# The end of the last block: the last half row is finished in two free banks, a quarter of a row each, with its earlier sum and x added ahead

## Chip, core and metric

One core of a Trainium2 chip. The metric is the device time of one execution in microseconds; the kernel before takes 622.09 us (median of the first three runs, 622.07 to 624.6). Each run also has a profile whose span is about 1.4 us shorter than its time. One run alone of a kernel on one core has the state "unknown"; kernels that were timed in several runs have the state "fast".

## The reference

```
xn = layernorm(x)                                   # x: [1, 2048, 1024] bf16
h_t = Lam_bar * h_(t-1) + B_bar xn_t                # a complex recurrence over 2048 steps
y   = 2 Re(C h) + xn * Dskip
act = a * tanh(softplus(a)),  a = xn w1 + b1        # w1: 1024 x 3584, w2: 3584 x 1024
out = x + y + act w2
```

## The kernel before

The rows are worked through in four blocks of 512. At the end of a block, `tail` sums the dense part (`act w2`) and the projection (`Re(C h)`) of eight *units* in the eight PSUM banks (the memory that TensorE sums into): unit u is row tile q = u//2 (128 rows) and half h = u%2 (512 of 1024 columns). The last steps of the projection (j = 5, 6, 7 with two components, so six matmuls a unit) are done row tile by row tile, so that VectorE can add x to a finished one and ScalarE's queue can store it while TensorE works on the next. In the last block the last row tile is finished in two halves: unit 6, then unit 7.

```python
        for j in range(NJ - njt):                       # the earlier steps, all units
            for ci in range(2):
                for u in range(8):
                    proj(j, ci, u, False)
        # ... cut
        def finish(q, lo, hi):
            # ... cut: src is one bank, or two as one row
            vop(lambda e: e.tensor_tensor(xr, src, xr, op=ALU.add), reads=b_src + [b_x], writes=[b_x])
            sem = s_out[i][q] if hi - lo > TB else DmaSem(nc, "d_end%d" % lo)
            out_events[i, q, lo] = AC.dma(lambda e: e.dma_start(out[0, r0:r0 + P, lo:hi], xr), sem, reads=[b_x])

        for q in range(NQ):
            units = [(2 * q, 2 * q + 1)]
            if blk == NB - 1 and q == NQ - 1:
                units = [(2 * q,), (2 * q + 1,)]        # the last row tile: unit 6, then unit 7
            for us in units:
                for j in range(NJ - njt, NJ):
                    for ci in range(2):
                        for u in us:
                            proj(j, ci, u, j == NJ - 1 and ci == 1)
                if len(us) == 1:
                    finish(q, (us[0] % 2) * TB, (us[0] % 2 + 1) * TB)
            if len(units) == 1:
                finish(q, 0, D)
```

`vop`, `PE.mm` and `AC.dma` put an instruction on the queue of VectorE, TensorE or ScalarE, with the waits that its data need. VectorE's queue runs in the order in which the program fills it.

## Time and profile before

In all views PE is TensorE (PEld its weight loads), DVE VectorE, ACT ScalarE, POOL GpSimd and SP SyncE; a q behind an engine means its queue. In a chain of waits, "issue" is time in which the engine waited for nothing that the profile shows; elsewhere in this text an *issue* is the work of a queue to start one transfer, and *landing* the moment when that transfer is reported complete.

The lines below are from the page of the kernel before: the span, each engine's busy time with its share, and the chain that ended last, by engine.

```profile
span 620.4 us, 7332 instructions
...
PE 613.4 (99%) x2905; PEld 287.6 (46%) x2961; DVE 465.6 (75%) x687; ACT 244.7 (39%) x158; POOL 49.9 (8%) x47
...
PE 96%; ACT 2%; DVE 1%; issue 1%; POOL 0%; DVEq 0%; POOLq 0%
```

TensorE is busy nearly all of the time. A change at the end of the last block can only touch what follows TensorE's last result. The next fence is the timeline from 616 us (start, duration, engine, line, operation, output<-inputs, shape, count; in brackets the engine's idle time before it and what ended it).

```profile
615.36 1.99 DVE L758 TENSOR_TENSOR xx<-ps,xx 128x1024 bf16<-128x1024 f32 x2 [1.36 <-PE ps L721]
615.80 2.10 PE L721 MATMUL ps<-CT,hT 128*128 128x512 bf16 x9
616.02 1.39 PEld L721 LDWEIGHTS ps<-CT,hT 128*128 128x128 bf16 x7
616.61 2.39 ACTq L760 DMA_DIRECT2D out_dram<-xx  x3
617.95 0.69 DVE L758 TENSOR_TENSOR xx<-ps,xx 128x512 bf16<-128x512 f32 x1 [0.60 <-PE ps L721]
```

The first line merges two adds: that of the third row tile (615.36, 1.22 us) and unit 6's (616.65, 0.69 us). Then VectorE is idle for 0.60 us until TensorE has finished unit 7, and adds its 512 columns from 617.95 to 618.64. The chain of waits ends the same way, with matmuls and then one add:

```profile
614.08 3.85 PE ps L721 x17
617.92 0.02 issue
617.95 0.69 DVE xx L758
```

The last two stores in the view of the issuing line (duration of the issue in ns, min/median/max; then time from the issue to landing):

```profile
L760 ACTq DMA_DIRECT2D out_dram<-xx x2: 339/339/339, 617.4 to 618.7; - x2
...
DMA to landing us min/median/max: 1.7/1.7/1.7
```

So the end is: last matmul result, 0.69 us of add, 0.03 us, 1.70 us of store (0.34 us of it the issue; the trace has landing at 620.37 for an issue at 618.67). The **tail**: from the start of the third row tile's add, which that row's last matmul releases, to the end of the span. Before, 620.412 - 615.356 = 5.06 us.

One more line of this profile is of use, from the timeline at the kernel's start: matmuls of 256 columns, of which the change will make twelve. 56 of them take 6.36 us; less the 0.27 us of one, that is 55 spacings of 111 ns on average (in the trace nearly all are 109 ns, and one is 183).

```profile
14.12 6.36 PE L502 MATMUL ps<-xnT,ring 128*128 128x256 bf16 x56
```

### The profile page before, as it was taken

What the parts mean: (1) busy time and instruction counts of PE and PEld (TensorE: products, weight loads), DVE (VectorE), ACT (ScalarE), POOL (GpSimd) and SP (SyncE); (2) the same over time, 40 slices, a digit from 0 to 9 for tenths busy, and PEclk for the clock granted to TensorE, in tenths of its full rate; (3) what the DMA queues carried; (4) which work ended last, traced back from release to release, by engine and by line L of the source; (5) the groups of instructions that cost most, each with busy time, mean ns of one, the idle gap of its engine ahead of it and who ended that gap; (6) DMA issues with size and microseconds to landing.
All of it is one profiled execution on the core that took longest, in us unless ns stands there. A gap on an engine that the chain in (4) does not pass through costs nothing.

```text
span 620.4 us, 7332 instructions
## 1 busy us (share of the span) xinstructions
PE 613.4 (99%) x2905; PEld 287.6 (46%) x2961; DVE 465.6 (75%) x687; ACT 244.7 (39%) x158; POOL 49.9 (8%) x47
## 2 busy tenths in 40 slices
PE   8999999999999999999999999999999999999998
PEld 8544444444444444444444444444444444444443
DVE  6899999999467599998147659999624856999603
ACT  5679995441079940000009992000001999000000
POOL 1998000000100000000010000000000000000000
PEclk9999999999999999999999999999999999999999
DMA  9999967740464301763065420285204542033001
GB/s 261 244 292 277 204 132 206 202 136 0 157 182 141 132 1 36 220 186 103 17 189 165 140 100 1 92 215 163 75 35 136 167 139 69 1 128 111 1 0 69
DMA packets 124332, 79.41 MB, mean 128 GB/s; under 512 B 48906, under 2 KB 106762, under 8 KB 124298
## 3 DMA queue, kind: packets, MB, share of 16 engines
q1 hardware_dynamic: 120800, 71.58, 42.4%
q10 hardware_dynamic: 2538, 4.21, 1.9%
q0 software_dynamic: 960, 3.15, 1.6%
q8 instruction: 24, 0.39, 0.3%
q14 instruction: 10, 0.08, 0.0%
HBM read 63.19 MB, written 4.19 MB: 109 GB/s over the span
## 4 chain that ended last, share of the span: by engine, by line
PE 96%; ACT 2%; DVE 1%; issue 1%; POOL 0%; DVEq 0%; POOLq 0%
PE ps L721 49%; PE ps L644 26%; PE ps L664 18%; PE ps L502 2%; PE ps L462 1%; ACT act L624 1%; ACT act L622 1%; ACT act L623 1%; DVE hb L651 0%; DVE act L629 0%; PE ps L383 0%; ACT L623 0%; DVE xx L436 0%; DVE xx L758 0%; DVE mt L434 0%
## 5 line engine op out<-in xcount | busy, mean ns | idle before, releaser
L721 PE MATMUL ps<-ring,act 128*128 128x512 bf16 x880 | 193.2, 379 | 0.8
L644 PE MATMUL ps<-xnT,ring 128*128 128x512 bf16 x832 | 182.7, 379 | 0.8
L622 ACT ACTIVATE act<-hb 128x3584 bf16<-128x3584 bf16 x16 | 50.9, 3183 | 244.2 <-DVE hb L651 243.7
L721 PEld LDWEIGHTS ps<-ring,act 128*128 128x128 bf16 x896 | 87.6, 98 | 105.8 <-DVE mt L669 0.3
L644 PEld LDWEIGHTS ps<-xnT,ring 128*128 128x128 bf16 x848 | 83.0, 98 | 99.8
L651 DVE TENSOR_SCALAR hb<-ps,par 128x512 bf16<-128x512 f32 x112 | 82.7, 747 | 55.1 <-PE ps L644 53.8
L664 PE MATMUL ps<-xnT,BT 128*128 128x512 bf16 x500 | 110.5, 379 | 0.6
L721 PE MATMUL ps<-CT,hT 128*128 128x512 bf16 x500 | 110.5, 379 | 0.6
L669 DVE TENSOR_TENSOR mt<-ps,tab 128x1024 bf16<-128x1024 f32 x64 | 75.3, 1219 | 13.3 <-PE ps L664 11.7
L664 PEld LDWEIGHTS ps<-xnT,BT 128*128 128x128 bf16 x512 | 50.1, 98 | 60.4
L721 PEld LDWEIGHTS ps<-CT,hT 128*128 128x128 bf16 x512 | 50.1, 98 | 60.4
L758 DVE TENSOR_TENSOR xx<-ps,xx 128x1024 bf16<-128x1024 f32 (+1 forms) x17 | 19.5, 1160 | 70.2 <-PE ps L721 70.1
L687 DVE TENSOR_TENSOR_SCAN hT<-cs,qi,hT 128x512 bf16<-128x512 f32 x48 | 58.9, 1268 | 0.0
L624 ACT ACTIVATE act<-act 128x3584 bf16<-128x3584 bf16 x16 | 51.0, 3190 | 0.2
L623 ACT ACTIVATE act<-act 128x3584 bf16<-128x3584 bf16 x16 | 51.0, 3190 | 0.2
L692 DVE TENSOR_TENSOR mt<-hT,tab 128x1024 bf16<-128x1024 bf16 x64 | 41.4, 688 | 1.1
L629 DVE TENSOR_TENSOR act<-act,hb 128x3584 bf16<-128x3584 bf16 x16 | 32.3, 2018 | 1.3 <-ACT act L624 1.3
L287 POOL DMA_DIRECT2D xx<-in_A_x_dram x12 | 6.7, 559 | 253.1 <-DVE xx L758 248.6
L598 ACT ACTIVATE ct<-CT,cs 128x512 f32<-128x512 bf16 x16 | 11.5, 718 | 28.8 <-DVE CT L600 24.5
L623 ACT ACT_TABLE_LOAD x16 | 20.5, 1283 | 0.3
L624 ACT ACT_TABLE_LOAD x16 | 20.5, 1283 | 0.3
L687 DVE TENSOR_TENSOR_SCAN hT<-cs,hT 128x512 bf16<-128x512 f32 x16 | 18.7, 1208 | 0.0
(78 smaller groups left out, 277.2 us busy)
## 6 DMA issues: line engine op xcount, KB each, us to landing
ring<-in_B_w_dram SPq DMA_DIRECT2D x112, 512.0 KB, 3.9
out_dram<-xx ACTq DMA_DIRECT2D x15, 256.0 KB, 2.1
xx<-in_A_x_dram POOLq DMA_DIRECT2D x12, 256.0 KB, 4.5
xx<-in_A_x_dram SPq DMA_DIRECT2D x3, 256.0 KB, 4.8
xx<-in_A_x_dram SPq DMA_DIRECT2D x2, 128.0 KB, 2.2
dsk<-in_A_Dskip_dram SPq DMA_DIRECT2D x1, 256.0 KB, 7.0
out_dram<-xx ACTq DMA_DIRECT2D x2, 128.0 KB, 1.7
xnT<-xn SPq DMA_TRANSPOSE x12, 4.5
```

Of the source, the lines that this page charges most:

```text
L622: aop(lambda e: e.activation(a, hs, AF.Exp), reads=[b_hb[g % 2]], writes=[b_act[g]])
L623: aop(lambda e: e.activation(a, a, AF.Ln, bias=1.0), reads=[b_act[g]], writes=[b_act[g]])
L624: aop(lambda e: e.activation(a, a, AF.Tanh), reads=[b_act[g]], writes=[b_act[g]])
L629: vop(lambda e: e.tensor_tensor(a, a, hs, op=ALU.mult), reads=[b_act[g], b_hb[g % 2]], writes=[b_act[g]])
L644: PE.mm(lambda e, k=k: e.matmul(ps[:, bank, :], lhsT=wt[:, k, fi * P:(fi + 1) * P], rhs=xnT[:, k, :], start=k == 0, stop=k == NK - 1), rea ...
L651: vop(lambda e: e.tensor_scalar(hb[:, hs, :], ps[:, bank, :], b1(f), None, op0=ALU.add), reads=[b_ps[bank], b_par], writes=[b_hbf[hs]])
L664: PE.mm(lambda e, j=j, ci=ci, k=k, bank=bank: e.matmul(ps[:, bank + ci, :], lhsT=BT[:, ci, j, k, :], rhs=xnT[:, k, :], start=k == 0, stop= ...
L669: vop(lambda e, s=s, u=u, j=j: e.tensor_tensor(mt[:, s, :, :], u, tab[:, s, j, :].unsqueeze(1).to_broadcast([P, 2, TB]), op=ALU.mult), rea ...
L687: vop(lambda e, ci=ci, init=init: e.tensor_tensor_scan(out=hT[:, ci, j, :], data0=cj("r", j).to_broadcast([P, TB]), data1=hT[:, ci, j, :], ...
L692: vop(lambda e, s=s: e.tensor_tensor(mt[:, s, :, :], hT[:, :, j, :], tab[:, s, j, :].unsqueeze(1).to_broadcast([P, 2, TB]), op=ALU.mult), ...
L721: PE.mm(lambda e: e.matmul(ps[:, u, :], lhsT=lhsT, rhs=rhs, start=st_, stop=last), reads=reads, writes=[b_ps[u]], first=st_, last=last)
L758: vop(lambda e: e.tensor_tensor(xr, src, xr, op=ALU.add), reads=b_src + [b_x], writes=[b_x])
```

## The change

The intent is to have less to do after the last matmul. Unit 7's sum so far (all but the last six matmuls) and x are added by VectorE into an f32 scratch tile. The last six steps go to banks 0 and 1, which are free by then, as two quarters of 256 columns: six matmuls for the first, six for the second. Each quarter is added to its part of the scratch and stored by itself, so only the second quarter's add and store follow the last matmul.

```diff
-                    proj(j, ci, u, False)
+                    proj(j, ci, u, blk == NB - 1 and u == 7 and j == NJ - njt - 1 and ci == 1)
 # ... cut
+        ends = blk == NB - 1
         for q in range(NQ):
+            units = (2 * q, 2 * q + 1) if not (ends and q == NQ - 1) else (2 * q,)
+            for j in range(NJ - njt, NJ):
+                for ci in range(2):
+                    for u in units:
+                        proj(j, ci, u, j == NJ - 1 and ci == 1)
+            finish(q, 0, len(units) * TB)
+        if ends:
+            tmp, b_tmp = ct[0]
+            b_x = b_xx[i][3].parts[1]
+            vop(lambda e: e.tensor_tensor(tmp[:], ps[:, 7, :], xx[:, i, 3, TB:D], op=ALU.add),
+                reads=[b_ps[7], b_x], writes=[b_tmp])
+            for h in range(2):
+                lo = TB + 256 * h
+                # ... six matmuls of 256 columns into bank h (cut)
+                vop(lambda e, h=h, lo=lo: e.tensor_tensor(
+                    xx[:, i, 3, lo:lo + 256], ps[:, h, 0:256], tmp[:, 256 * h:256 * h + 256], op=ALU.add),
+                    reads=[b_ps[h], b_tmp], writes=[b_end[h]])
+                out_events["end", h] = AC.dma(...)      # 64 KB (cut)
```

More of the change, by code (lines that the diff above doesn't have):

```diff
@@ L714, in build_kernel @@
     out_events = {}
+    b_end = [Buf("end%d" % h) for h in range(2)]
     def tail(blk):
@@ L732, in proj, with proj_quarter @@
             acc(u, hT[:, ci, j, q * P:(q + 1) * P], CT[:, ci, j, h * TB:(h + 1) * TB], [b_hT[ci][j], b_CT[j]], last)
+        def proj_quarter(j, ci, bank, lo, st_, last):
+            PE.mm(lambda e: e.matmul(ps[:, bank, 0:256], lhsT=hT[:, ci, j, 3 * P:4 * P], rhs=CT[:, ci, j, lo:lo + 256],
+                                     start=st_, stop=last),
+                  reads=[b_hT[ci][j], b_CT[j]], writes=[b_ps[bank]], first=st_, last=last)
         njt = 1 if blk == 0 else 3
@@ L746, in tail, with store @@
                 for u in range(8):
-                    proj(j, ci, u, False)
+                    proj(j, ci, u, blk == NB - 1 and u == 7 and j == NJ - njt - 1 and ci == 1)
         i = blk % 2
+        def store(q, lo, hi, sem):
+            r0 = blk * TB + q * P
+            b_x = b_xx[i][q] if hi - lo > TB else b_xx[i][q].parts[lo // TB]
+            out_events[i, q, lo] = AC.dma(lambda e: e.dma_start(out[0, r0:r0 + P, lo:hi], xx[:, i, q, lo:hi]),
+                                          sem, reads=[b_x])
@@ L750, in finish @@
         def finish(q, lo, hi):
+            bank, n = 2 * q + lo // TB, (hi - lo) // TB
+            b_x = b_xx[i][q] if n > 1 else b_xx[i][q].parts[lo // TB]
             xr = xx[:, i, q, lo:hi]
-            bank, r0 = 2 * q + lo // TB, blk * TB + q * P
-            b_x = b_xx[i][q].parts[lo // TB] if hi - lo <= TB else b_xx[i][q]
-            if hi - lo > TB:
-                src, b_src = ps[:, bank:bank + 2, :].rearrange("p a t -> p (a t)"), b_ps[bank:bank + 2]
-            else:
-                src, b_src = ps[:, bank, lo % TB:lo % TB + hi - lo], b_ps[bank:bank + 1]
@@ L758, in finish @@
-            vop(lambda e: e.tensor_tensor(xr, src, xr, op=ALU.add), reads=b_src + [b_x], writes=[b_x])
-            sem = s_out[i][q] if hi - lo > TB else DmaSem(nc, "d_end%d" % lo)
-            out_events[i, q, lo] = AC.dma(lambda e: e.dma_start(out[0, r0:r0 + P, lo:hi], xr), sem, reads=[b_x])
-        for q in range(NQ):
-            units = [(2 * q, 2 * q + 1)]
-            if blk == NB - 1 and q == NQ - 1:
-                units = [(2 * q,), (2 * q + 1,)]
-            for us in units:
+            src = ps[:, bank:bank + n, :].rearrange("p a t -> p (a t)")
@@ new lines, in finish @@
+            vop(lambda e: e.tensor_tensor(xr, src, xr, op=ALU.add), reads=b_ps[bank:bank + n] + [b_x], writes=[b_x])
+            store(q, lo, hi, s_out[i][q])
+        ends = blk == NB - 1
+        for q in range(NQ):
+            units = (2 * q, 2 * q + 1) if not (ends and q == NQ - 1) else (2 * q,)
[4 more added lines that the diff above has]
+            finish(q, 0, len(units) * TB)
@@ L767, in tail @@
+        if ends:
[5 more added lines that the diff above has]
+                lo = TB + 256 * h
                 for j in range(NJ - njt, NJ):
                     for ci in range(2):
-                        for u in us:
-                            proj(j, ci, u, j == NJ - 1 and ci == 1)
@@ L771, in tail @@
-                if len(us) == 1:
-                    finish(q, (us[0] % 2) * TB, (us[0] % 2 + 1) * TB)
-            if len(units) == 1:
-                finish(q, 0, D)
+                        proj_quarter(j, ci, h, lo, j == NJ - njt and ci == 0, j == NJ - 1 and ci == 1)
+                vop(lambda e, h=h, lo=lo: e.tensor_tensor(
+                    xx[:, i, 3, lo:lo + 256], ps[:, h, 0:256], tmp[:, 256 * h:256 * h + 256], op=ALU.add),
+                    reads=[b_ps[h], b_tmp], writes=[b_end[h]])
@@ L775, in tail @@
+                r0 = blk * TB + 3 * P
+                out_events["end", h] = AC.dma(lambda e, lo=lo, r0=r0: e.dma_start(
+                    out[0, r0:r0 + P, lo:lo + 256], xx[:, i, 3, lo:lo + 256]), DmaSem(nc, "d_end%d" % h), reads=[b_end[h]])
         if blk + 2 < NB:
```

## The prediction

> **What bounds the kernel now.** TensorE. The busy table has PE at 99% of a 620.4 us span, at full granted clock; the chain that ended last is 96% PE, 1% VectorE. The change can only move what follows the last matmul. The timeline of the last 10 us shows that tail: the last 128x512 matmul runs 617.53 to 617.91; the last VectorE add (128x512, f32 PSUM + bf16) 617.95 to 618.64 (0.69 us); ScalarE's queue issues the last 128 KB store at 618.67 (0.34 us); it lands at 620.37, 1.70 us after issue. The tail is about 2.5 us, 0.4% of the time, so 2% is out of reach.
>
> **What the change does.**
> - PE: the last six 128x512 matmuls (216 ns apart) become twelve 128x256. Early in this kernel 128x256 matmuls run 109 ns apart, so 1.31 us against 1.30: the last PE result stays near 617.93.
> - VectorE: one add of 512 columns becomes three: 512 columns PSUM + x into an f32 scratch, then two of 256. The Trainium skill, "VectorE: DVE Perf Modes", section on the TRN2 errata, gives (N+151)/0.96 ns for an fp32 tensor_tensor add; the trace agrees at 512 (691 ns measured), so I estimate 424 ns for 256.
> - DMA: the last 128 KB store becomes two of 64 KB with 512 B rows. Packets take 85 ns at 2 KB and 47 ns at 1 KB in the trace; extrapolated (estimate) 28 ns at 512 B. With 8 packets an engine the last store saves 0.15 of its 1.70 us.
>
> **The critical path.** If the scratch add were out of the way, the last add would be 0.27 us shorter and the store 0.15 us: 0.4 us gained. But VectorE works in order, and the scratch add stands behind the add of unit 6, which can't start before 616.65. Independent adds of 1024 columns follow each other at 1.14 us, so of 512 at about 0.61 (estimate). Scratch add: 617.26 to 617.95. First quarter (waits for the scratch, 0.04 us as between dependent adds elsewhere): 617.99 to 618.42. Second (0.34 later): 618.33 to 618.76, where before ended at 618.64. So VectorE, not PE, ends last: the second quarter's bank is ready about 0.4 us before VectorE, and the add ends about 0.1 us LATER. The first quarter's issue holds ScalarE's queue from 618.45 to 618.79, so the last issue comes at 618.8, 0.13 to 0.15 later than before. The shorter store gives 0.15 back. Net: 0.0 us, -0.2 to +0.2.
>
> **Prediction.** 622.1 us, range 621.4 to 623.0 (mostly the spread of executions: 622.07 to 624.6 before). Faster by over 2%: 0.5%; within 2%: 99%; slower by over 2%: 0.5%.
>
> **What would show each step right or wrong.** In the timeline of the last 5 us: twelve 128x256 matmuls about 109 ns apart, ending within 0.05 us of before; the scratch add right behind unit 6's add; quarter adds of 0.42 us, back to back, the second not waiting for PE; VectorE ending at 618.7 to 618.8; two issues of 0.34 us touching; the last store landing in 1.5 to 1.6 us. The chain of waits should end in several VectorE adds instead of one.
>
> **What would make it wrong.** Weight loads (98 ns each) failing to hide behind 109 ns matmuls would delay the last bank, with 0.4 us of slack. Two small stores on the same DMA engines may interfere, or 512 B packets take as long as 1 KB ones: +0.15 us. If the scratch add ran earlier than I read from the order: -0.4 us.

## The result

Before 622.26 us median (6 runs, 622.07 to 624.6), changed 622.14 us median (6 runs, 621.88 to 624.65): the same. The ratio is 0.9998, with a 95% interval of 0.9977 to 1.0019. (A ratio is the mean time of one kernel's fast runs over that of the other's of the same rounds, so it is not quite the ratio of the medians.)

The page of the changed kernel, the same lines:

```profile
span 620.5 us, 7405 instructions
...
PE 616.3 (99%) x2967; PEld 288.1 (46%) x2967; DVE 466.3 (75%) x689; ACT 244.8 (39%) x158; POOL 49.9 (8%) x47
...
PE 99%; DVE 0%; POOL 0%; issue 0%; DVEq 0%; POOLq 0%
```

The 62 additional matmuls are mostly records that were missing before; the change itself adds six. The timeline from 616 us:

```profile
615.29 1.99 DVE L767 TENSOR_TENSOR xx<-ps,xx 128x1024 bf16<-128x1024 f32 x2 [1.36 <-PE ps L722]
615.73 0.81 PE L722 MATMUL ps<-CT,hT 128*128 128x512 bf16 x3
615.95 0.10 PEld L722 LDWEIGHTS ps<-CT,hT 128*128 128x128 bf16 x1
616.17 1.41 PEld L736 LDWEIGHTS ps<-CT,hT 128*128 128x128 bf16 x12
616.38 1.47 PE L736 MATMUL ps<-CT,hT 128*128 128x256 bf16 x12
616.54 1.10 ACTq L759 DMA_DIRECT2D out_dram<-xx  x2
617.19 0.68 DVE L782 TENSOR_TENSOR ct<-ps,xx 128x512 f32<-128x512 f32 x1
617.98 0.76 DVE L789 TENSOR_TENSOR xx<-ps,ct 128x256 bf16<-128x256 f32 x2
618.43 0.82 ACTq L793 DMA_DIRECT2D out_dram<-xx  x2
```

Here everything until 616.5 is 0.07 us earlier than before (615.29 against 615.36), which has nothing to do with the end. Seen from there: the twelve small matmuls end at 617.85, so TensorE is as fast as before. But no line of VectorE after the first has a bracket: it goes from the third row tile's add and unit 6's add with hardly a pause to the scratch add and the quarters, and ends at 618.73, where TensorE's last result was there 0.88 us earlier. In the chain of waits, the matmuls stop at unit 6:

```profile
613.95 2.60 PE ps L722 x12
616.56 0.02 issue
616.58 0.69 DVE xx L767
617.27 0.61 DVE ct L782
617.88 0.03 issue
617.91 0.02 DVEq L131
617.93 0.04 issue
617.98 0.76 DVE xx L789 x2
```

Four adds stand in the chain instead of one. The two small stores, in the view of their line:

```profile
L793 ACTq DMA_DIRECT2D out_dram<-xx x2: 338/391/444, 618.4 to 618.8; - x2
...
DMA to landing us min/median/max: 1.6/1.6/1.7
```

One issue took 338 ns, the other 444; one store landed in 1.59 us, the other in 1.70. In the trace the slow one is the second, the one that counts. The tail is 620.550 - 615.286 = 5.26 us: **0.21 us longer than before**. That is 0.03% of the time and can't be seen in it.

### The profile page after: what moved, and what is told of

Its sections match the earlier page's. It is cut to its first block, busy times and chain, and to the rows that moved or that the text cites. A ratio compares the mean times of both kernels' runs of the same rounds, so it can differ in the third digit from the quotient of the medians.

```text
span 620.5 us, 7405 instructions
## 1 busy us (share of the span) xinstructions
PE 616.3 (99%) x2967; PEld 288.1 (46%) x2967; DVE 466.3 (75%) x689; ACT 244.8 (39%) x158; POOL 49.9 (8%) x47
## 4 chain that ended last, share of the span: by engine, by line
PE 99%; DVE 0%; POOL 0%; issue 0%; DVEq 0%; POOLq 0%
PE ps L722 49%; PE ps L644 29%; PE ps L664 18%; PE ps L502 2%; PE ps L462 1%; PE ps L383 0%; DVE xx L789 0%; DVE xx L767 0%; DVE ct L782 0%; DVE xnT L396 0%; POOL ident L330 0%; POOL ident L329 0%; DVE par L486 0%; PE ps L467 0%; POOL kon L333 0%
```

## The experiments

Two questions were open: whether the 0.21 us are real, and which of the terms makes them. Theory A: VectorE's queue order (the scratch add stands behind unit 6's add, though its data are there much sooner). Theory D: on ScalarE's queue, an issue that directly follows another is slower, and this takes back what the smaller store gains. Rivals: the small stores gain nothing in themselves (B, E), or the quarter matmuls and their banks eat the gain (C).

All runs gave correct results. This table has all of them, from the traces, in us; the first two columns are counted from the start of the third row tile's add. Each row is one trace; the changed kernel alone has two, and they agree to 0.007 us in the tail. The timed runs of e3 to e8 were one each (622.18 to 624.21 us, state "unknown") and give no verdict. e1 to e4 ran on one chip, e5 to e8 on another.

| kernel | last VectorE add ends | last issue starts | its issue takes | issue to landing | tail |
|---|---|---|---|---|---|
| before | 3.28 | 3.31 | 0.339 | 1.698 | 5.056 |
| changed | 3.45 | 3.52 | 0.444 | 1.696 | 5.264 |
| e1 changed, again | 3.44 | 3.52 | 0.444 | 1.689 | 5.257 |
| e2 scratch add early | 3.03 | 3.06 | 0.338 | 1.588 | 4.693 |
| e3 one store | 3.44 | 3.47 | 0.339 | 1.714 | 5.231 |
| e4 first store from SyncE | 3.44 | 3.47 | 0.338 | 1.594 | 5.111 |
| e5 early, half not split | 3.28 | 3.31 | 0.338 | 1.708 | 5.065 |
| e6 before, end split | 3.34 | 3.43 | 0.442 | 1.689 | 5.159 |
| e7 scratch add in the middle | 3.08 | 3.32 | 0.459 | 1.708 | 5.070 |
| e8 as e7, first store from SyncE | 3.08 | 3.11 | 0.338 | 1.585 | 4.742 |

The expectations of e1 to e4 count the tail from the start of unit 6's add instead, which is about 1.30 us less; I convert where I compare.

### e1: the changed kernel again

No edit.

> The changed kernel unaltered, to learn how far the tail repeats. Tail = from the start of unit 6's VectorE add (which the last matmul of unit 6 releases) to the end of the span: before 620.41 - 616.65 = 3.76 us, changed 620.55 - 616.58 = 3.97 us. Every theory expects 3.97 within 0.03 here, and a time of 621.9 to 622.4 us. If the tail comes out below 3.85, the 0.21 us that separate the two traces are chance and there is nothing to explain.

Tail from unit 6's add 621.240 - 617.278 = 3.96 us, against 3.97: the end repeats to 0.01 us, and the 0.21 us are real. The time does not repeat: median 623.41 us in 6 runs (622.19 to 624.56), outside the 621.9 to 622.4 expected; ratio to before 1.0013 (0.9997 to 1.0029). So two sets of runs of one kernel have medians 1.3 us apart, six times what is to be explained. Where this comes from is told below.

### e2: the scratch add early

```diff
         ends = blk == NB - 1
+        if ends:
+            tmp, b_tmp = ct[0]
+            ...vop(... tmp[:], ps[:, 7, :], xx[:, i, 3, TB:D] ...)
         for q in range(NQ):
 ...
         if ends:
-            tmp, b_tmp = ct[0]
-            ...vop(... tmp[:], ps[:, 7, :], xx[:, i, 3, TB:D] ...)
```

> The scratch add is moved on VectorE's queue ahead of all the finishing adds of the last block; nothing else. Theory A (the queue's order costs it: the scratch add stands behind unit 6's add, so VectorE ends last): the second quarter add is now released by PE, ends about 0.43 us earlier than in the changed kernel; the two issues no longer touch, the last store lands in 1.59 us; tail about 3.97 - 0.43 - 0.03 - 0.11 = 3.40 us, i.e. 0.36 below before. Rival B (small stores with 512 B rows cost what they save, whatever VectorE does: the last one lands in 1.70): tail about 3.51. Rival C (the quarter matmuls or the two banks are what eats the gain, the order is harmless): tail stays at 3.97. Time about 0.5 us below the repeat of the changed kernel under A, hardly clear of noise.

Tail from unit 6's add 620.763 - 617.365 = 3.40 us, as theory A said; from the third row tile's 4.69, 0.57 less than the changed kernel and 0.36 less than before. The scratch add ran 7.77 us before the third row tile's add, where in the changed kernel it ran 1.90 us after it. VectorE had been idle there for 23 us:

```profile
608.30 0.69 DVE L774 TENSOR_TENSOR ct<-ps,xx 128x512 f32<-128x512 f32 x1 [23.44 <-PE ps L722]
```

The chain of waits of this run ends with TensorE and one small add again:

```profile
617.33 1.32 PE ps L736 x12
618.65 0.02 issue
618.67 0.42 DVE xx L790
```

This also clears the quarter matmuls: twelve take 1.32 us in the chain, and the last add starts right after them. The two issues of the quarters:

```profile
L794 ACTq DMA_DIRECT2D out_dram<-xx x2: 338/398/458, 618.5 to 619.1; - x2
```

Here the first is the slow one: it starts 0.05 us after the end of unit 6's issue and takes 0.458 us. The last starts after a pause of 0.20 us, takes 0.338 us and lands in 1.588 us. Rivals B and C fall. The time, 622.74 us median in 6 runs (ratio to before 1.0000, 0.9984 to 1.0016), can't show 0.36 us.

### e3: one store for both quarters

```diff
-                out_events["end", h] = AC.dma(... xx[:, i, 3, lo:lo + 256] ..., reads=[b_end[h]])   # in the loop
+            out_events["end", 0] = AC.dma(... xx[:, i, 3, TB:D] ..., reads=b_end)                 # after it
```

> The changed kernel, but both quarters leave in one 128 KB store after the second add. Theory D (the second small store pays for following the first directly: its issue took 0.44 instead of 0.34 us, and so it landed in 1.70, not 1.59): one store issues in 0.34 and lands in 1.70, and starts about 0.05 earlier because the queue is free: tail 3.92, so splitting the store gained nothing at all. Rival E (the split of the store does save 0.1 us or more): tail 4.05 or more.

Tail from unit 6's add 621.323 - 617.386 = 3.94 us, expected 3.92 under D and 4.05 or more under E. Cutting the store in two gained nothing in the changed kernel; it cost 0.03 us, little more than the scatter of the landings (1.689 to 1.714 us in such runs).

### e4: the first quarter's store from SyncE's queue

```diff
-                out_events["end", h] = AC.dma(lambda e, lo=lo, r0=r0: e.dma_start(
+                out_events["end", h] = (SP, AC)[h].dma(lambda e, lo=lo, r0=r0: e.dma_start(
```

> The changed kernel, but the first quarter's store is issued from SyncE's queue, which is idle, the second from ScalarE's as now. If it is ScalarE's own sequencer that stretches the second issue to 0.44 us (theory D1): second issue 0.34 us, starting 0.05 us earlier, landing in 1.59: tail about 3.81. If it is what all queues share in making descriptors or moving data (D2): the second issue is still stretched, or the store still takes 1.70 from issue to landing: tail about 3.92.

Tail from unit 6's add 620.926 - 617.110 = 3.82 us, expected 3.81 under D1 and 3.92 under D2. The two issues even overlapped (SyncE's ran from 618.95 to 619.32, ScalarE's started at 619.29), and ScalarE's took its 0.338 us all the same:

```profile
L793 SPq DMA_DIRECT2D out_dram<-xx x1: 361/361/361, 619.0 to 619.0; - x1
L793 ACTq DMA_DIRECT2D out_dram<-xx x1: 338/338/338, 619.3 to 619.3; - x1
```

So the stretch belongs to one engine's own queue.

### e5: scratch early, the half not split

The kernel of e2, but bank 0 takes the whole half: six matmuls of 512 columns, one add, one store.

```diff
-            for h in range(2):
-                ...six matmuls of 256 columns into bank h, add 256 columns, store 64 KB
+            ...six matmuls of 512 columns into bank 0
+            vop(lambda e: e.tensor_tensor(xx[:, i, 3, TB:D], ps[:, 0, :], tmp[:], op=ALU.add), ...)
+            ...store 128 KB
```

> From here the tail is counted from the start of the add of the third row of tiles (released by that row's last matmul in every kernel) to the end of the span: before 5.06 us, changed 5.26, repeat 5.26, scratch add early 4.69. This kernel has the scratch add early, but the last half row stays whole: six 128x512 matmuls into one free bank, one add of 512 columns, one 128 KB store. Theory A (the gain of the early version comes from the smaller last add and store; the scratch only makes the split possible): last add 0.69 us as in before, tail 5.06, within 0.03. Rival F (taking part of the sum and x out of the last add is itself worth something): below 4.95.

Tail 5.065 us, as before (5.056). Rival F falls: taking part of the sum and x out of the last add is worth nothing by itself, since that add takes 0.691 us in both kernels. What e2 gains, it gains by the smaller last add and store.

### e6: only the end split

The kernel before, its last add and store cut in two; the matmuls stay as they were.

```diff
-                    finish(q, (us[0] % 2) * TB, (us[0] % 2 + 1) * TB)
+                    ...unit 6 as before; for unit 7:
+                        for h in range(2):
+                            lo = TB + 256 * h
+                            vop(... xx[:, i, 3, lo:lo + 256], ps[:, 7, 256 * h:256 * h + 256], ...)
+                            out_events["end", h] = AC.dma(...)
```

> The kernel before, with only the last add and the last store cut into two quarters; matmuls and bank as before, no scratch. Tail counted as in the run with the whole half. Theory D (an issue that directly follows another on ScalarE's queue takes 0.44 instead of 0.34 us and its store loses the 0.11 us it had gained): second add ends 0.76 after the last PE result, its issue starts at 0.84 behind the first's, lands 1.69 later: tail 5.16, 0.10 worse than before. If touching issues cost nothing: 5.05. If cutting the end pays by itself: 4.96 or less.

Tail 5.159 us, as theory D said, with nearly the same two durations as in the changed kernel (338 and 444) though VectorE does other things:

```profile
L783 ACTq DMA_DIRECT2D out_dram<-xx x2: 338/390/442, 620.7 to 621.0; - x2
```

### e7 and e8: the scratch add in the middle

e7 is the kernel of e2 with the scratch add between the third row tile's add and unit 6's; e8 is e7 with the edit of e4.

```diff
             finish(q, 0, len(units) * TB)
+            if ends and q == NQ - 2:
+                ...scratch add
```

> The scratch add stands between the third row's add and unit 6's add, where VectorE would otherwise work back to back: it delays unit 6's add by about 0.45 us, but the second quarter's add is only 0.09 us later than in the early version. Worked out from spacings seen so far: scratch add starts 1.14 us after the third row's, unit 6's add 0.61 later, first quarter 0.61 later, second 0.34 later, ending 3.12 us after the third row's add started. If VectorE's end decided the rest: tail 4.78. Theory D (touching issues): unit 6's, the first quarter's and the second quarter's issues all stand back to back on ScalarE's queue and the last two take 0.45 us: last issue at 3.35, lands 1.69 later, tail 5.09. If they queue but without stretching: 4.87.

> As the run with the scratch add in the middle, but the first quarter's store is issued from SyncE's queue. Theory D: ScalarE's queue is free when the second quarter's add ends, its issue takes 0.34 and lands in 1.59: tail 4.79, 0.30 below the middle run with the same VectorE times. If it isn't ScalarE's queue but VectorE or the data movement that costs the 0.30: tail stays above 5.0.

VectorE ends at the same time in both (3.08 us after the third row tile's add, 0.37 earlier than in the changed kernel), and yet the tails are 5.07 and 4.74. The issues of e7 and then of e8:

```profile
L794 ACTq DMA_DIRECT2D out_dram<-xx x2: 446/452/459, 618.5 to 619.0; - x2
...
DMA to landing us min/median/max: 1.7/1.7/1.7
```

```profile
L794 SPq DMA_DIRECT2D out_dram<-xx x1: 360/360/360, 619.1 to 619.1; - x1
L794 ACTq DMA_DIRECT2D out_dram<-xx x1: 338/338/338, 619.4 to 619.4; - x1
...
DMA to landing us min/median/max: 1.6/1.6/1.6
```

In e7 three issues stand back to back on ScalarE's queue and the last two are stretched; in e8 none is. The 0.33 us between them is 0.21 us of later start and 0.12 us of slower store. The Trainium skill, "DMA: Bandwidth & Descriptors", section "Issuing engines are not separate DMA queues", says that issuing from several engines only saves the sequencer's time for initiating, which is usually small beside the transfer. The trace agrees about what is saved; at the end of a kernel it was 0.33 of 5.07 us.

### Why the time can't show it

Against the kernel before, all traces are shifted by a constant amount from about 100 us on, to within 0.04 us, until the last adds. In e6 it is 2.26 us, in e1 0.63, in e5 1.19. The shift arises at the start: in e1 and e5 within the first 15 us, in e6 mostly between 42 and 100 us. There, a line of the waits of e6 and one of its TensorE timeline:

```profile
DVE stats L405 <- DMA xx<-in_A_x_dram: 1.7, 1, 1.7
```

```profile
93.80 11.40 PE L722 MATMUL ps<-ring,act 128*128 128x512 bf16 x51 [1.21 <-DVE mt L669]
```

VectorE waited 1.7 us for a load of the next block's x, and TensorE waited in turn for VectorE; the kernel before has no such wait in that stretch of its profile. In e1 and e5 it is TensorE that waits in the first 15 us, for a load of weights (0.4 and 1.1 us), and the kernel before does not. So the moment when loads land differs from trace to trace, and with it the starts, by up to 2.3 us. That these loads account for the whole spread of the timed runs was not tested.

## Why the prediction was right

**The time.** 622.1 us predicted, 622.14 measured, within 2% as said. That the tail is 0.4% of the time was enough for this; the range (621.4 to 623.0) is so wide beside the effect that the hit tests none of the steps below. The traces do.

**TensorE.** Right: the twelve matmuls are 109 ns apart in the trace and end as before (2.57 us after the start of the third row tile's add, before 2.55). The Trainium skill's "TensorE: Matmul & The Clock Gate", section "Back-to-back issue gap", gives N/2.4 + 2.5 ns as the gap of isolated matmuls for a warm clock, which is 109 for 256 columns.

**VectorE becomes last, because of its queue's order.** Right, and shown by e2: moving that one add takes 0.42 us off VectorE's end and 0.57 us off the tail. The same page of the skill (section "Architectural detail") says that VectorE works strictly first in, first out; the trace agrees, as the scratch add, with data ready by 608 us, started at 617.19.

**VectorE's end.** About 0.12 us later predicted (618.76 against 618.64), 0.165 measured. The quarter adds took 425 and 415 ns (424 estimated). The adds follow each other at 0.61 us (512 columns) and 0.34 (256), as estimated. The mis-sized term is the gap between the scratch add and the first quarter: 0.04 us expected, 0.105 measured, in which the chain shows a wait instruction of VectorE's sequencer of its own (the first quarter waits for TensorE and for the scratch).

**"The shorter store gives 0.15 back."** This step failed. The last store took 1.696 us, as long as the one of twice the size before. The packets were shorter as estimated (27 ns, against 47 before), and a small store that follows no other at once landed in 1.585 to 1.594 us (the first quarter's in the changed kernel, the last in e2, e4, e8), so it is worth 0.11 us. But the last issue came 0.04 us behind another on the same queue and took 0.444 us instead of 0.338. The prediction foresaw the queue being busy ("two issues of 0.34 us touching") but not that touching makes the second one longer. e3, e4, e6 and e8 show it from four sides. The packets in the traces show where the time goes: those of the last store take 0.35 us in the changed kernel and in e2 alike (0.51 for the whole half before, so 0.16 is saved, as predicted), but they start 0.95 us after the issue's start in the changed kernel and 0.84 in e2 and before. The prediction's other worry, that two small stores slow each other's packets, did not come true. The last 0.05 between 0.16 and 0.11 is lost after the last packet: 0.40 us to the landing in e2, 0.35 before; why is open.

**The net.** 0.0 us expected, -0.2 to +0.2; measured +0.208 in the tail, just outside. The last issue came 0.21 us later (0.13 to 0.15 predicted). The sum: VectorE's end +0.165, the busy queue +0.046, the store -0.002. With the scratch add early, all of the gain that the change was made for is there: 0.36 us, of which 0.25 is VectorE's end and 0.11 the store; the prediction had 0.4.

The version of e2 has the shortest tail. The timed runs can't tell it from the other two.

## What to carry to other kernels

An operation that was taken out of the critical end by data is out of it only if it is also issued earlier: look at where it stands in its engine's queue, since a ready instruction behind a waiting one is not ready. Cutting the last store in two paid here only where the last issue did not come directly behind another on the same queue (e2, and e4 against e3; not in the changed kernel and e6). Two queues for the two pieces saw to that in e4. And before polishing the last 2.5 us, compare two runs of one kernel: here their starts differ by more than the whole effect.

## What the Trainium skill lacked or had wrong

- "TensorE: Matmul & The Clock Gate", section "Back-to-back issue gap", has about 131 ns per matmul for a sustained stream of weight loads and matmuls of 512 columns. This kernel's stream, a weight load with every matmul at full clock, runs at 216 ns (the isolated value that the page also gives); at 256 columns 109 ns.
- "DMA: Bandwidth & Descriptors" has no time in ns for an issue on ScalarE's queue, nor anything on issues that follow each other there. At the end of these kernels a store's issue takes 0.338 us, and 0.442 to 0.459 us where it starts within 0.05 us after the end of the issue before it on the same queue; after a pause of 0.20 us (e2) it was 0.338 again. It is no rule for every transfer: at the start of the kernel before, three small loads (2 to 7 KB) stand just as close behind others on ScalarE's queue and take 0.29 to 0.32 us. Why is open.
- The same page's fit, 2.0 us and bytes over 436 GB/s (section "Anatomy of one DMA"), is for transfers issued from GpSimd; the page has none for stores from ScalarE's queue. Here they took 1.70 us for 128 KB and 1.59 us for 64 KB.
- "VectorE: DVE Perf Modes", section on the TRN2 errata: the page has (N+151)/0.96 ns measured at 512 and 2048 columns. It also holds here at 256 (424 to 425 ns) and 1024 (1223 to 1226), with one input in PSUM and bf16 in the mix, but an add directly behind another can be recorded up to 13 ns shorter (681 at 512, 411 to 415 at 256).
